# Loading the first pair of units by SyncE as fp32 and rounding it on the chip, in a fused attention and GELU kernel

## The chip, the cores and the metric

One Trainium2 chip, one of its cores. The metric is the device time of one execution in microseconds (us). The kernel before takes 132.57 us (median of 3 runs, 132.43 to 132.61). The profiled span of such a run is 130.3 us; the difference lies outside the profile.

## The reference

Inducing-point attention over `x` (4 batches of 12480 rows of 128), then an expert layer with exact GELU:

```python
def _attn_ref(x, inducing):
    ...                                  # scale = 1/sqrt(C), I = inducing for every batch
    def mab(q, kv):
        s = scale * (q @ kv.transpose(0, 2, 1))
        s = s - s.max(-1, keepdims=True)
        a = np.exp(s)
        a /= a.sum(-1, keepdims=True) + 1e-09
        return a @ kv
    h = mab(I, x)
    return mab(x, h).astype(np.float32)

def _moe_ref(x, w_in, w_out):            # x: the 49920 rows that the attention gives
    h = x @ w_in                         # 128 -> 2048
    g = 0.5 * h * (1.0 + erf(h * inv_sqrt2))
    return (g @ w_out).astype(np.float32)
```

The attention gives so small values that the kernel computes the expert layer from the 32 rows of `h` alone, with a check at the end. What matters here is the traffic: 25.6 MB of `x` in, 25.6 MB out, 2.1 MB of weights.

## The kernel before

`x` is worked on in units of 2048 rows, two units (a pair) to a tile of 128 partitions x 32 rows. GpSimd loads each pair in one transfer of 2.1 MB that rounds to fp16 on its way. For the first pair alone, SyncE loads the first half as fp32, and VectorE rounds it in two instructions:

```python
    def a_load(u):
        nc.gpsimd.dma_start(out=x_tile(u), in_=u.rows_of(x_rows))
...
    x_first = sb.tile([128, 32, 128], FP32, tag="o", bufs=OBUFS)
    x_pair = x_tile(units[0][0])
    src = units[0][0].rows_of(x_rows)
    nc.sync.dma_start(out=x_first[:, :16, :], in_=src[:, :16, :])
    nc.gpsimd.dma_start(out=x_pair[:, 16:, :], in_=src[:, 16:, :])
    a_load(units[0][2])
...
    ind_s = consts.tile([M, C], FP32)
    nc.scalar.dma_start(out=ind_s, in_=inducing)
...
    def a_cast(c0, engine):
        evacuate(engine, x_pair[:, c0 : c0 + 8, :], x_first[:, c0 : c0 + 8, :])
```

The order of all later work comes from a planner in the kernel: each piece is added with its cost in us, the buffers that it takes and gives, and, if it moves data, the length of the move. The planner runs the pieces through a model of engines and queues and emits them in that order, which is then pinned. A change of the loads therefore rearranges the whole program:

```python
    def add_load(u):
        if not loads:
            p = plan.add((0, 0), {"SP": 0.01}, lambda e: None, takes=["o"], move=LOAD_US)
            for c0 in (0, 8):
                p = plan.add((0, 1), {"DVE": 0.7, "ACT": 1.1},
                             lambda e, c0=c0: a_cast(c0, e), [p],
                             gives=["o"] if c0 == 8 else [])
            loads.append(p)
        elif len(loads) == 1:
            loads.append(plan.add((0, 1), {"POOL": 0.55}, lambda e: None,
                                  takes=["xh"], move=LOAD_US))
        elif u.first:
            ...
```

After building, the first transfers are moved ahead of the start barrier, each engine's to just before its first instruction of a given kind:

```python
def loads_ahead(nc):
    ...
    for engine, n, kind in (
        (ET.SP, 1, mybir.InstDrain),
        (ET.Activation, 1, mybir.InstDrain),
        (ET.Pool, 2, mybir.InstEventSemaphore),
    ):
        ...
```

Stores go by SyncE, one for each pair (2.1 MB) and, in the last batch, one for each unit (1.05 MB).

## Time and profile before

| | kernel before |
|---|---|
| time | 132.57 us |
| compute over at | 118.8 us of 130.3 |
| busy: PE, DVE, ACT, POOL | 76%, 70%, 59%, 50% |
| DMA time: GpSimd's queue (q0) + SyncE's (q1) | 50.1% + 48.9% of the span |
| HBM traffic | 27.7 MB read, 25.6 MB written |

PE is TensorE (PEld its weight loads), DVE is VectorE, ACT is ScalarE and POOL is GpSimd. The lines behind the table are in the prediction. Three things on reading them: the DMA row of the 40 slices is the mean of the 16 DMA engines; a line of a stretch has, after its length, the busy time and number of instructions of PE, PEld, DVE, ACT and POOL, then the granted clock, the DMA share and GB/s written; and in such a stretch the DMA share can exceed 1, because a packet counts whole where it begins and packets overlap (up to 25 at once in this trace). Eight filler matmuls, whose results nobody reads, stand at PE's start; the text comes back to them.

### The profile page before, as it was taken

Reading aid. Unit: us, or ns where it says so; the run is one execution under the profiler, and the core shown is the slowest. Engines: PE = TensorE matmul, PEld = TensorE weight load, DVE = VectorE, ACT = ScalarE, POOL = GpSimd, SP = SyncE. Lnnn points to the kernel's source line nnn. Section 1 sums busy time; section 2 is a strip of 40 time slices with the busy share of each in tenths; the row PEclk is TensorE's granted clock in tenths of the full one; section 3 lists DMA queues with packets and bytes.
Section 4 is the critical chain, followed back from the end, with each engine's and each line's share of the span. In section 5 each row is a group of like instructions: output and inputs, shape, how many; then the busy total and the mean of one; then the engine's idle time right before and its main releaser. Section 6 shows DMA issues by size and latency. Waiting matters only on the chain. (4 is left out here: it accounts for less than half of the span.)

```text
span 130.3 us, 3507 instructions
## 1 busy us (share of the span) xinstructions
PE 99.2 (76%) x1365; PEld 57.5 (44%) x1365; DVE 91.6 (70%) x265; ACT 77.1 (59%) x177; POOL 65.2 (50%) x85
## 2 busy tenths in 40 slices
PE   0954878549999999999789899999996698860000
PEld 0342656349465547656544664655453413310000
DVE  1836257432699997999999977999999757993000
ACT  3007064416756888578968889798996285960000
POOL 7910113019453836895753679765198842770000
PEclk9999599965799999999999999999999657998555
DMA  4999999999999999999999999999999999999993
GB/s 131 311 228 214 211 206 211 229 209 214 224 199 219 221 211 322 322 380 377 302 324 330 310 220 288 340 367 418 443 424 419 407 453 418 405 428 430 428 418 125
DMA packets 5666, 40.17 MB, mean 308 GB/s; under 512 B 624, under 2 KB 1936, under 8 KB 2192
## 3 DMA queue, kind: packets, MB, share of 16 engines
q0 software_dynamic: 2848, 13.30, 50.1%
q1 hardware_dynamic: 2752, 26.61, 48.9%
q8 instruction: 11, 0.18, 0.5%
q10 hardware_dynamic: 48, 0.02, 0.1%
q14 instruction: 7, 0.06, 0.1%
HBM read 27.67 MB, written 25.56 MB: 409 GB/s over the span
## 5 line engine op out<-in xcount | busy, mean ns | idle before, releaser
L702 POOL TENSOR_TENSOR pair<-pair,rr 128x512 f32<-128x512 f32 x26 | 26.8, 1042 | 20.6 <-ACT pair L365 17.7
L686 PE MATMUL at<-q,e 128*128 128x512 f16 (+1 forms) x104 | 33.4, 389 | 3.8 <-DVE xT L363 1.2
L377 PE MATMUL tr<-identity_h,xh 128*128 128x128 f16 x392 | 30.3, 232 | 3.3 <-DMA xh<-in_x_dram 3.3
L377 PEld LDWEIGHTS <-xh 128*128 128x128 f16 x392 | 25.2, 105 | 9.9 <-DMA xh<-in_x_dram 4.8
L363 DVE COPY xT<-tr 128x1024 f16<-128x1024 f16 (+1 forms) x36 | 22.6, 645 | 8.9 <-PE tr L377 8.3
L365 ACT ACTIVATE xT<-tr 128x1024 f16<-128x1024 f16 (+1 forms) x16 | 15.7, 980 | 16.5 <-PE tr L377 16.5
L717 DVE TENSOR_TENSOR pair<-at,rr 128x512 f32<-128x512 f32 x36 | 23.3, 676 | 1.1 <-PE at L686 0.4
L287 POOL DMA_DIRECT2D xh<-in_x_dram x15 | 8.3, 555 | 21.4 <-DMA xh<-in_x_dram 14.2
L403 ACT ACTIVATE e<-s 128x512 f16<-128x512 f32 (+1 forms) x28 | 15.3, 546 | 5.6 <-PE s L391 5.1
L638 ACT ACTIVATE e<-s 128x512 f16<-128x512 f32 (+1 forms) x28 | 15.0, 563 | 3.6 <-PE s L626 1.8
L365 ACT ACTIVATE pair<-at 128x512 f32<-128x512 f32 x26 | 15.6, 600 | 1.6 <-PE at L686 1.0
L686 PEld LDWEIGHTS <-e 128*128 128x128 f16 (+1 forms) x104 | 8.7, 103 | 10.3 <-issue 6.9
L417 DVE STREAM_TRANSPOSE e1t<-e 128x256 int32<-128x256 int32 (+1 forms) x28 | 11.1, 399 | 3.0 <-ACT e L403 2.9
L572 POOL TENSOR_TENSOR pt<-pt 128x512 f32<-128x512 f32 (+4 forms) x20 | 12.0, 602 | 2.1 <-DVE rr L661 0.7
L425 PE MATMUL hun<-xh,e1t 128*32 128x128 f16 x392 | 10.7, 225 | 3.1 <-DVE e1t L417 3.0
L717 DVE TENSOR_TENSOR o<-at,rr 128x512 f32<-128x512 f32 (+1 forms) x19 | 10.5, 580 | 3.0 <-PE at L686 2.6
L391 PE MATMUL s<-xT,indT 128*32 128x512 f16 (+1 forms) x108 | 10.5, 376 | 1.6 <-ACT xT L365 0.8
L626 PE MATMUL s<-xT,hT 128*32 128x512 f16 (+1 forms) x100 | 10.2, 417 | 0.5 <-DVE rr L661 0.5
L425 PEld LDWEIGHTS <-e1t 128*32 128x32 f16 x392 | 6.3, 97 | 8.9 <-DVE e1t L417 6.5
L702 POOL TENSOR_TENSOR o<-o,rr 128x512 f32<-128x512 f32 x7 | 7.3, 1042 | 5.4 <-ACT o L365 3.0
L650 PEld LDWEIGHTS <-e 128*128 128x128 f16 (+1 forms) x104 | 5.6, 99 | 4.4 <-issue 1.7
L650 PE MATMUL r<-strand,e 128*128 128x4 f16 (+1 forms) x104 | 6.8, 168 | 0.0
(76 smaller groups left out, 100.6 us busy)
## 6 DMA issues: line engine op xcount, KB each, us to landing
out_dram<-pair SPq DMA_DIRECT2D x8, 2048.0 KB, 15.1
xh<-in_x_dram POOLq DMA_DIRECT2D x11, 1024.0 KB, 28.1
out_dram<-o SPq DMA_DIRECT2D x6, 1024.0 KB, 10.7
out_dram<-spent SPq DMA_DIRECT2D x1, 2048.0 KB, 18.3
x_first<-in_x_dram SPq DMA_DIRECT2D x1, 1024.0 KB, 5.2
xh<-in_x_dram POOLq DMA_DIRECT2D x1, 512.0 KB, 7.1
w_in_h<-in_moe_w_in_dram POOLq DMA_DIRECT2D x1, 512.0 KB, 17.4
w_out_h<-in_moe_w_out_dram POOLq DMA_DIRECT2D x1, 512.0 KB, 19.4
```

The costliest lines, as they stand in the source:

```text
L363: nc.vector.tensor_copy(out=out, in_=in_)
L365: nc.scalar.activation(out=out, in_=in_, func=AF.Copy)
L377: nc.tensor.transpose(tr[:, c - c0, : u.p], xh[: u.p, c, :], identity_h[: u.p, : u.p])
L403: nc.scalar.activation(out=e1[: u.p, : u.nc // 2, :, :], in_=s1[: u.p, : u.nc, :].rearrange("r (a b) i -> r a i b", b=2), func=AF.Exp, sca ...
L417: nc.vector.transpose(out=pairs(e1t)[: u.p, :n], in_=pairs(e1)[: u.p, :n])
L425: nc.tensor.matmul(bt.hun[32 * j : 32 * j + 32, :], e1t[: u.p, c // 2, :, c % 2], xh[: u.p, c, :], start=u.idx == 0 and c < 4, stop=c + 4 ...
L572: nc.gpsimd.tensor_tensor(out=bt.pt[:, :, :, :half], in0=bt.pt[:, :, :, :half], in1=bt.pt[:, :, :, half : 2 * half], op=ALU.add,)
L638: nc.scalar.activation(out=e2[: u.rows, : u.cols], in_=s2[: u.rows, : u.cols], func=AF.Exp, scale=SCALE,)
L650: nc.tensor.matmul(r2[: u.p, ci, : u.nj], e2[: u.rows, ci * u.p : (ci + 1) * u.p], strand[: u.rows, : u.nj], start=True, stop=True,)
L686: nc.tensor.matmul(at[: u.p, : u.nj, :], e2[: u.rows, ci * u.p : (ci + 1) * u.p], bt.q[: u.rows, : u.nj, :], start=True, stop=True,)
L702: nc.gpsimd.tensor_tensor(out=part, in0=part, in1=rr2[: u.p, ci, : u.nj].unsqueeze(2).broadcast_to([u.p, u.nj, 128]), op=ALU.mult,)
L717: nc.vector.tensor_tensor(out=ov[: u.p, ci, :, :], in0=at[: u.p, : u.nj, :], in1=rr2[: u.p, ci, : u.nj].unsqueeze(2).broadcast_to([u.p, u. ...
```

## The change

SyncE loads the whole first pair as fp32 in two transfers, issued ahead of everything else on SyncE, and the second half is rounded on the chip too. GpSimd begins with the second pair.

```diff
-    nc.gpsimd.dma_start(out=x_pair[:, 16:, :], in_=src[:, 16:, :])
+    nc.sync.dma_start(out=x_first[:, 16:, :], in_=src[:, 16:, :])
     a_load(units[0][2])
+    a_load(units[0][4])
...
-        if not loads:
-            p = plan.add((0, 0), {"SP": 0.01}, lambda e: None, takes=["o"], move=LOAD_US)
-            for c0 in (0, 8):
+        if len(loads) < 2:
+            c = 16 * len(loads)
+            p = plan.add(..., takes=[] if loads else ["o", "xh"], move=LOAD_US)
+            for c0 in (c, c + 8):
...                                   (the planner's other lines follow suit)
-        (ET.SP, 1, mybir.InstDrain),
+        (ET.SP, 2, mybir.InstRegisterMove),
```

More of the change, by code (lines that the diff above doesn't have):

```diff
@@ L771, in add_load @@
     def add_load(u):
-        if not loads:
-            p = plan.add((0, 0), {"SP": 0.01}, lambda e: None, takes=["o"], move=LOAD_US)
-            for c0 in (0, 8):
+        if len(loads) < 2:
+            c = 16 * len(loads)
+            p = plan.add(
+                (0, 0),
+                {"SP": 0.01},
+                lambda e: None,
+                takes=[] if loads else ["o", "xh"],
+                move=LOAD_US,
+            )
+            for c0 in (c, c + 8):
                 p = plan.add(
-                    (0, 1),
+                    (0, 1 + c),
                     {"DVE": 0.7, "ACT": 1.1},
@@ L779, in add_load @@
                     [p],
-                    gives=["o"] if c0 == 8 else [],
+                    gives=["o"] if c0 == 24 else [],
                 )
             loads.append(p)
-        elif len(loads) == 1:
+        elif u.b == 0 and u.idx == 2:
             loads.append(
                 plan.add(
-                    (0, 1), {"POOL": 0.55}, lambda e: None, takes=["xh"], move=LOAD_US
+                    (0, 1), {"POOL": 0.55}, lambda e: None, takes=["xh"], move=2 * LOAD_US
                 )
@@ L793, in add_load @@
                     {"POOL": 0.55},
-                    lambda e: None if u.b == 0 and u.idx == 2 else a_load(u),
+                    lambda e: None if u.b == 0 and u.idx == 4 else a_load(u),
                     takes=["xht" if u.tail else "xh"],
@@ L999 @@
             nc,
-            {ET.SP: 0, ET.DVE: 26, ET.Activation: 0, ET.Pool: 12, ET.PE: 15},
+            {ET.SP: 0, ET.DVE: 26, ET.Activation: 0, ET.Pool: 11, ET.PE: 15},
         )
```

## The prediction

> **What bounds the kernel now.** I read the page's 40 slices first, because the share of busy time by engine (PE 76%, DVE 70%) names no bound.
>
> ```profile
> PE   0954878549999999999789899999996698860000
> DVE  1836257432699997999999977999999757993000
> ACT  3007064416756888578968889798996285960000
> DMA  4999999999999999999999999999999999999993
> GB/s 131 311 228 214 211 206 211 229 209 214 224 199 219 221 211 322 322 380 377 302 324 330 310 220 288 340 367 418 443 424 419 407 453 418 405 428 430 428 418 125
> ```
>
> The reader is to see that DMA is at 9 in every slice but the first and the last, while every compute engine has slices far below 9, and that in the last three to four slices (some 10 us) no engine works at all and the DMA still moves some 420 GB/s. GB/s counts what is written: a load that rounds fp32 to fp16 on its way shows half of what it reads, so 210 in slices 3 to 15 is 420 read, the same as the 405 to 453 of the pure stores from slice 28 on. Second, the queues:
>
> ```profile
> q0 software_dynamic: 2848, 13.30, 50.1%
> q1 hardware_dynamic: 2752, 26.61, 48.9%
> HBM read 27.67 MB, written 25.56 MB: 409 GB/s over the span
> ```
>
> The two add to 99% of the span. Per HBM megabyte: GpSimd's queue reads 26.6 MB (twice 13.30) in 0.501 x 130.3 = 65.3 us, 2.45 us each; SyncE's moves 26.61 MB in 0.489 x 130.3 = 63.7 us, 2.39 us each. Third, the busy time by stretch, which says where the DMA is not full (the columns end in clock, DMA share, GB/s):
>
> ```profile
> 0.00:1.00 1.00, 0.00 (x0) 0.00 (x0) 0.00 (x0) 0.00 (x0) 0.20 (x4) 1.00 0.00 0
> 1.00:2.00 1.00, 0.00 (x0) 0.00 (x0) 0.18 (x1) 0.00 (x0) 0.93 (x2) 1.00 0.50 92
> 2.00:3.00 1.00, 0.00 (x0) 0.00 (x1) 0.16 (x2) 0.87 (x1) 0.93 (x4) 1.00 0.84 260
> 3.00:4.00 1.00, 0.97 (x3) 0.46 (x4) 0.60 (x7) 0.41 (x1) 1.00 (x3) 1.00 0.96 401
> 120.00:125.00 5.00, 0.00 (x0) 0.00 (x0) 0.00 (x0) 0.00 (x0) 0.00 (x0) 0.50 1.01 428
> 125.00:128.00 3.00, 0.00 (x0) 0.00 (x0) 0.00 (x0) 0.00 (x0) 0.00 (x0) 0.50 0.87 363
> 128.00:130.30 2.30, 0.00 (x0) 0.00 (x0) 0.00 (x0) 0.00 (x0) 0.00 (x0) 0.50 0.18 69
> ```
>
> Only the first 3 to 4 us and the last 3 us are not full; every 2 us stretch between has a share of 0.94 or more. Last, the chain of waits, to see that compute is not what ends the run:
>
> ```profile
> 117.61 0.60 DVE hit L438 x8
> 118.25 0.22 PE tot_ps L969 x2
> 118.70 0.14 DVE failed L979
> ```
>
> Compute is over at 118.84, and the last store is issued at 118.0. What ends the run is about 9 us of queued stores, some 4 MB at 428 GB/s. So the kernel is 53.2 MB of HBM traffic at some 425 GB/s (125 us), a start of about 2 us and a close of about 3 us.
>
> **What the Trainium skill says.** (1) "DMA: Bandwidth & Descriptors", section "Issuing engines are not separate DMA queues": transfers issued by any engine run on the same 16 DMA engines, so starting them from several engines saves only issuing time. The trace agrees: 0.501 + 0.489 is a shared, full resource, not two. (2) Same page, "Specifications": a ceiling of 435 GB/s, and a first-byte latency of about 1 us for GpSimd's path, 0.6 us for SyncE's. The 428 here is at that ceiling; the first latencies can't be read singly, but no byte lands in the first 1 us. (3) Same page, "Queues, rings and completion order": each DMA engine takes turns between the queues that have work, packet by packet. Here 26.6 MB / 2848 and 26.61 MB / 2752 give 9.3 and 9.7 KB of HBM traffic a packet, so two active queues should get half each. (4) Same page, "SWDGE vs HWDGE vs iDMA": a cast in the transfer is to be had from GpSimd only, which is why SyncE's half comes as fp32 and is rounded on the chip.
>
> **The change, part by part.**
>
> Second half of the first pair (1.05 MB of HBM reads) moved from GpSimd's queue to SyncE's. HBM bytes stay the same; at the two rates above it saves 1.05 x (2.45 - 2.39) = 0.06 us of DMA time.
>
> SyncE's loads come ahead of its register moves. Before, SyncE's issue stands behind four of them; ScalarE's first issue stands behind none:
>
> ```profile
> 0.14 0.42 ACTq L305 DMA_DIRECT2D ind_s<-in_inducing_dram  x1
> 0.26 0.38 SPq L295 DMA_DIRECT2D x_first<-in_x_dram  x1
> 1.07 0.72 POOL L296 DMA_DIRECT2D xh<-in_x_dram  x1 [0.61 <-issue]
> 1.78 0.54 POOL L287 DMA_DIRECT2D xh<-in_x_dram  x1
> ```
>
> SyncE should issue at about 0.14, so 0.12 us earlier. As nothing else feeds the DMA then, and the DMA is full afterwards, this counts in full: -0.12 us. The second SyncE issue takes 0.38 us more before the start barrier; SyncE waits 0.8 us there now (its own waits say so), so it is free. GpSimd still has two issues ahead of the barrier (second and third pair now), so its first bytes and the identity that it makes after them don't move.
>
> The end tapers over some 3 us (share 0.87, then 0.18), so the 16 engines don't finish together. If the late ones are late because of GpSimd's transfers, 1.05 of 26.6 MB less takes 4% of some 2.5 us: -0.1 us, an estimate from the taper and the least certain term.
>
> Two more roundings of 128x1024, at 0.72 us on VectorE (the two now take 1.37 us together). They lie at 10 to 12 us, where VectorE is at 0.3 to 0.7 of a slice: nothing on the path.
>
> What moves early on: the first half lands as now (about 5.3 us). All transposes of the first pair now wait for GpSimd's half, because the first carries that wait, and begin at 8.23; in the changed order they wait for the roundings alone, so the first half begins at about 6.1. Its second half shares the DMA with GpSimd's second pair, so it needs twice its 2.45 us: 5.3 + 4.9 = 10.2 us, and some 0.7 us of rounding, against 8.2 now: 2.5 to 3 us later. The second pair has the same 4.2 MB ahead of and in it, so it lands at about 13.5 as now. The order of PE puts half a second-pair unit ahead of the first gather, so PE is up to one unit (about 2 us) behind at 13.6. It catches up while loads bound it, or the first store leaves up to 2 us later than 45.3. Neither is on the path: by 20 us the loads issued are some 15 MB and those served some 7.5 MB.
>
> Sum: -0.06 - 0.12 - 0.1 = -0.28 us: 132.57 becomes 132.3.
>
> **The rivals.** First, the earlier start of compute carries through (transposes 2.1 us earlier, up to -2 us: 130.5). For it: PE and ScalarE idle up to 6 us for data early on. Against: compute ends 9 us before the run does, and a gain of 2 us there would make the queue of stores deeper, not the end earlier. Second, the later second half and the new order (stores and the three engines' work are rearranged all along) leave the DMA dry somewhere: +1 to +2 us, about 134. For it: at 74 to 78 us GB/s falls to 224 to 240, the mark of loads alone, so the stores' queue is then empty, and if loads were finished earlier a gap would open. Against: the loads still last until about 89 us (the last is issued at 53.1 and such take up to 36.8 us to land), and the backlog of stores stays at about 3 MB or more (7 us) from 90 us on. Third, the last store is now one of 1 MB, behind the small one instead of ahead of it: if the last tile were finished over 7 us later the drain would follow compute, +1 us and more; I see no reason for so much. Fourth, more traffic written into the chip (1.05 MB instead of 0.52) costs DMA time: if what is written set the rate, loads that round would have gone faster than 210 GB/s written; so no.
>
> **Range and chances.** Executions of the kernel before spread by 0.18 us, the sum of my terms is 0.28, and a reshuffled schedule may shift the mix of loads and stores by some tenths either way. I take 131.5 to 132.8 as the range, with more room on the fast side since the start may gain more than 0.12 us. Over 2% would need 2.65 us, nearly the whole start or a gap that no stretch hints at: 0.02 for faster, 0.02 for slower, 0.96 within.
>
> **What would show it.** Right: DMA share near 1.0 from 3 us on; the software queue at 12.8 MB and the hardware one at 27.7; SyncE's first issue at about 0.14 us; first transposes at about 6 us, the two late roundings at 10 to 12 us, the second pair's transposes at 13 to 14; compute done 6 to 11 us before the end. Wrong: a 2 us stretch in the middle with a share under 0.9, compute ending within 4 us of the end, or a taper at the end that is gone or twice as long (then the engines' imbalance is worth more than I gave it).

## The result, and the profile after

The changed kernel takes 132.46 us (median of 5 runs, 132.11 to 132.82) against 132.57 us (132.43 to 132.61); the ratio is 0.9995 with a 95% interval of 0.9974 to 1.0016. Measured again later on one chip with other kernels it was 132.27 us against 132.53 us, ratio 0.9981 (0.9955 to 1.0007). A ratio here is the mean time of one kernel's fast runs over that of the other's of the same rounds, so not quite the ratio of the medians. Neither interval leaves 1: the change is worth nothing that can be told from zero, nor from the 0.28 us predicted; the medians are 0.1 and 0.3 us lower.

The queues of the page, in the changed kernel:

```profile
q1 hardware_dynamic: 2896, 27.66, 51.1%
q0 software_dynamic: 2704, 12.78, 48.3%
HBM read 27.67 MB, written 25.56 MB: 408 GB/s over the span
```

Half of the pair has changed sides (0.52 MB as written less on q0, 1.05 MB more on q1), the sum is still 99% of the span, and the HBM traffic is the same.

Busy time by stretch in the changed kernel (the last columns are clock, DMA share, GB/s written):

```profile
1.00:2.00 1.00, 0.00 (x0) 0.00 (x0) 0.19 (x1) 0.00 (x0) 0.94 (x2) 1.00 1.14 229
2.00:3.00 1.00, 0.00 (x0) 0.00 (x0) 0.17 (x2) 0.00 (x0) 0.92 (x4) 1.00 0.91 312
...
125.00:128.00 3.00, 0.00 (x0) 0.00 (x0) 0.00 (x0) 0.00 (x0) 0.00 (x0) 0.50 0.83 347
128.00:130.30 2.30, 0.00 (x0) 0.00 (x0) 0.00 (x0) 0.00 (x0) 0.00 (x0) 0.50 0.13 53
```

Against the same stretches in the prediction: from 1 to 3 us, 541 KB are moved instead of 352, so the start is some 190 KB ahead, 0.45 us at 425 GB/s. At the other end the taper is hardly smaller (0.83 and 0.13 instead of 0.87 and 0.18), and the span is the same 130.3 us. But each is one execution, and both took 132.41 us; for the kernel before that is 0.16 us under its median, so the equal spans don't show that nothing came out. More was gained at the start than predicted; how much of it is in the time stays open.

The timeline of the first 13 us of the changed kernel:

```profile
0.00 0.39 SPq L295 DMA_DIRECT2D x_first<-in_x_dram  x1
0.12 0.38 ACTq L306 DMA_DIRECT2D ind_s<-in_inducing_dram  x1
0.44 0.42 SPq L296 DMA_DIRECT2D x_first<-in_x_dram  x1
...
4.41 0.28 PE L308 MATMUL indT_ps<-identity,ind_s 32*128 32x32 f32 x1 [4.41 <-DMA ind_s<-in_inducing_dram]
4.63 3.59 PE L360 MATMUL dim<-blank 128*128 128x512 f16 x8
4.74 0.19 DVE L310 CAST indT<-indT_ps 128x32 f16<-128x32 f32 x1 [1.59 <-PE indT_ps L308]
6.71 0.68 DVE L364 CAST xh<-x_first 128x1024 f16<-128x1024 f32 x1
8.02 1.81 PE L378 MATMUL tr<-identity_h,xh 128*128 128x128 f16 x16
12.36 0.69 DVE L364 CAST xh<-x_first 128x1024 f16<-128x1024 f32 x1 [1.80 <-DMA x_first<-in_x_dram]
```

SyncE now issues 0.26 us earlier, ahead of ScalarE's small load of the inducing points. That load, of 16 KB, lands 4.2 us after its issue instead of 2.8. PE's first matmul at 4.41 us (3.03 before) and with it VectorE's `indT` at 4.74 us wait for it. In VectorE's program the constants and the first rounding stand after `indT`, so that rounding begins at 6.71 us (5.50 before) and ends at 7.39. But it is PE itself that is late: its eight fillers stand after its first matmul, one every 0.43 us from 4.63 us, and the first transposes follow them without a gap at 8.02 us, not at 6.1 as predicted and hardly earlier than 8.24 before. The second half is rounded at 12.36 us; predicted was a landing at 10.2.

### The profile page after: what moved, and what is told of

Same layout as the page of the kernel before. It is cut to its first block, busy times and chain, and to the rows that moved or that the text cites. A ratio compares the mean times of both kernels' runs of the same rounds, so it can differ in the third digit from the quotient of the medians.

```text
span 130.3 us, 3513 instructions
## 1 busy us (share of the span) xinstructions
PE 98.2 (75%) x1365; PEld 59.1 (45%) x1365; DVE 89.1 (68%) x262; ACT 80.5 (62%) x188; POOL 63.1 (48%) x82
## 3 DMA queue, kind: packets, MB, share of 16 engines
q1 hardware_dynamic: 2896, 27.66, 51.1%
## 5 line engine op out<-in xcount | busy, mean ns | idle before, releaser
L703 POOL TENSOR_TENSOR pair<-pair,rr 128x512 f32<-128x512 f32 x25 | 26.1, 1048 | 22.5 <-ACT pair L366 22.3
L378 PE MATMUL tr<-identity_h,xh 128*128 128x128 f16 x392 | 31.2, 236 | 5.5 <-DMA xh<-in_x_dram 5.2
L378 PEld LDWEIGHTS <-xh 128*128 128x128 f16 x392 | 26.2, 107 | 11.5 <-DMA xh<-in_x_dram 6.0
L364 DVE COPY xT<-tr 128x1024 f16<-128x1024 f16 (+1 forms) x32 | 20.9, 657 | 9.4 <-PE tr L378 9.1
L366 ACT ACTIVATE xT<-tr 128x1024 f16<-128x1024 f16 (+1 forms) x20 | 19.0, 958 | 11.5 <-PE tr L378 11.4
L718 DVE TENSOR_TENSOR pair<-at,rr 128x512 f32<-128x512 f32 x37 | 24.0, 679 | 0.8 <-PE s L627 0.2
L287 POOL DMA_DIRECT2D xh<-in_x_dram x15 | 8.5, 575 | 22.8 <-DMA xh<-in_x_dram 11.3
L366 ACT ACTIVATE pair<-at 128x512 f32<-128x512 f32 x25 | 15.0, 599 | 0.9 <-PE at L687 0.4
L718 DVE TENSOR_TENSOR o<-at,rr 128x512 f32<-128x512 f32 (+1 forms) x17 | 9.7, 592 | 0.7 <-PE at L687 0.3
L703 POOL TENSOR_TENSOR o<-o,rr 128x512 f32<-128x512 f32 x6 | 6.2, 1039 | 5.7 <-ACT o L366 3.3
L711 ACT ACTIVATE o<-at,rr 128x128 f32<-128x128 f32 (+1 forms) x24 | 7.2, 396 | 1.0 <-PE at L687 1.0
```

The source lines that it names most:

```text
L364: nc.vector.tensor_copy(out=out, in_=in_)
L366: nc.scalar.activation(out=out, in_=in_, func=AF.Copy)
L378: nc.tensor.transpose(tr[:, c - c0, : u.p], xh[: u.p, c, :], identity_h[: u.p, : u.p])
L703: nc.gpsimd.tensor_tensor(out=part, in0=part, in1=rr2[: u.p, ci, : u.nj].unsqueeze(2).broadcast_to([u.p, u.nj, 128]), op=ALU.mult,)
L718: nc.vector.tensor_tensor(out=ov[: u.p, ci, :, :], in0=at[: u.p, : u.nj, :], in1=rr2[: u.p, ci, : u.nj].unsqueeze(2).broadcast_to([u.p, u. ...
```

## The experiments

Eleven runs were made (one of them the changed kernel again), all correct. Ratios are to the kernel before, run on the same chip in the same rounds. An execution more than 1.5% above the fastest of its kernel is called slow; where a time is judged, fast runs alone are used. A profile is one execution.

**1. More traffic.** SyncE loads 1.05 MB more, into a part of a tile that nobody reads (made from the kernel before):

```diff
     nc.gpsimd.dma_start(out=x_pair[:, 16:, :], in_=src[:, 16:, :])
+    nc.sync.dma_start(out=x_first[:, 16:, :], in_=src[:, 16:, :])
...
-        (ET.SP, 1, mybir.InstDrain),
+        (ET.SP, 2, mybir.InstDrain),
```

> The kernel before with an extra load by SyncE of 1.05 MB of fp32 into a part of a tile that nothing reads. Theory (the DMA's total work is the bound): 1.05 MB at 2.4 us a MB, so 2.3 to 2.6 us more than the kernel before, about 135.0 us, ratio 1.018. Rival (a chain of compute is the bound and the DMA has room): under 0.5 us more.

Measured: 135.22 us against 132.48 us, ratio 1.0211 (1.0183 to 1.0238), so 2.8 us more. The added transfer costs its whole DMA time and a little over. Compute came later too (first transposes at 11.3 us), but it was over at 122.65 us of 132.7, with 10.1 us of stores still to go. The DMA's total work is the bound; the rival is out.

**2. Compute later.** Each filler matmul at PE's start is issued twice (made from the changed kernel):

```diff
-        nc.tensor.matmul(dim, blank[:, :128], blank, start=True, stop=True)
+        for _ in range(2):
+            nc.tensor.matmul(dim, blank[:, :128], blank, start=True, stop=True)
```

> The changed kernel with each of the eight filler matmuls at PE's start issued twice, so PE is free for the first transposes 8 x 0.43 = 3.4 us later; all other instructions stand in the same order. Theory (compute has room of 6 us and more everywhere): the first transposes begin at about 11.5 us and the time stays within 0.3 us of the changed kernel. Rival (what compute gains or loses at the start is carried to the end): 2 to 3.4 us more.

Measured: 132.47 us, ratio 0.9993 (0.9964 to 1.0022), the time of the changed kernel. The delay is 2.0 us instead of the 3.4 expected. PE's timeline shows why:

```profile
4.81 5.37 PE L361 MATMUL dim<-blank 128*128 128x512 f16 x16
10.01 1.06 PE L379 MATMUL tr<-identity_h,xh 128*128 128x128 f16 x16
```

The first eight fillers start every 0.43 us, the second eight every 0.22 us, so sixteen take 5.2 us and not twice 3.4; the transposes follow them without a gap at 10.01 us instead of 8.02. Nothing of it arrives at the end: compute is over at 117.9 us, 1.1 us before the changed kernel's. A start of compute that is 2 us later does not move the time.

**3. SyncE behind its register moves.** Only the place of the two loads is undone (made from the changed kernel):

```diff
-        (ET.SP, 2, mybir.InstRegisterMove),
+        (ET.SP, 2, mybir.InstDrain),
```

> The changed kernel with both SyncE loads put back behind SyncE's four register moves, nothing else moved. Theory A (the DMA is the bound and a byte moved earlier at the start is kept to the end): SyncE issues at about 0.26 us, the first bytes come 0.25 us later, and the time is 0.2 to 0.3 us above the changed kernel, so 0.1 to 0.2 us above the kernel before (ratio about 1.001). Theory B (the gain at the start is lost again before the end, because the last bytes come from the slowest of the 16 DMA engines): the same as the changed kernel within 0.15 us. Beside this, if it is the order of the issues that delays the small load of the inducing points (ScalarE's issue would now be ahead of SyncE's), that load lands at about 3 us instead of 4.4, the roundings begin at about 5.5 us instead of 6.7 and the first transposes about 1.2 us earlier than in the changed kernel, with no effect on the time.

Measured: 132.37 us against 132.48 us, ratio 0.9991 (0.9970 to 1.0012). The head start is gone but for 0.05 MB at 20 us, and the time is not higher; but theory A's ratio of 1.001 lies in the interval as well as theory B's, so this run decides between them no more than 0.1 us can be told from nothing. The side question is settled: ScalarE's issue, at 0.14 us, is now ahead of SyncE's at 0.26, the small load lands in 2.6 us, the first rounding begins at 5.55 us and the first transposes at 6.58, where the fillers end. It is the order of the issues that delays the small load, and that has no effect on the time: with experiment 2, neither 2 us later nor 1.4 us earlier transposes move it.

**4. SyncE ahead, without the second transfer.** One word of the change alone (made from the kernel before):

```diff
-        (ET.SP, 1, mybir.InstDrain),
+        (ET.SP, 1, mybir.InstRegisterMove),
```

> The kernel before with one thing of the change alone: SyncE's first load ahead of its register moves. Theory A: the first bytes come 0.25 us earlier and the time falls by 0.2 to 0.3 us (132.3). Theory B: the first bytes come earlier, the time stays within 0.1 us of the kernel before. The small load of the inducing points should land later than 2.9 us if its place behind SyncE's issue is what delays it.

Measured: 132.65 us against 132.48 us, ratio 1.0008 (0.9988 to 1.0029): no gain of the 0.2 to 0.3 us of theory A, although the first bytes come earlier (the interval does allow the prediction's 0.12 us). The small load lands 4.6 us after its issue, as expected. In the profile, the stretches from 5 to 7 us show where the earlier bytes go. The kernel before:

```profile
5.00:6.00 1.00, 1.00 (x4) 0.38 (x3) 0.91 (x11) 0.00 (x0) 1.00 (x3) 1.00 1.04 213
6.00:7.00 1.00, 0.79 (x2) 0.00 (x0) 0.86 (x2) 0.00 (x0) 0.37 (x1) 1.00 1.06 209
```

The kernel with SyncE's single load ahead:

```profile
5.00:6.00 1.00, 1.00 (x4) 0.42 (x4) 0.56 (x8) 0.00 (x0) 1.00 (x3) 1.00 0.89 180
6.00:7.00 1.00, 1.00 (x4) 0.32 (x3) 0.87 (x6) 0.00 (x0) 0.24 (x1) 1.00 1.05 152
```

In these 2 us GpSimd's queue is all but alone in both. It reads 2 x (213 + 209) = 844 KB in the one and 2 x (180 + 152) = 664 KB in the other: 180 KB are lost while the DMA goes over from SyncE's queue to GpSimd's. By 20 us (twice the bytes of q0 and once those of q1 in the stretch from 0 to 20 us) the kernel before has moved 7.45 MB, this one 7.35 and the changed kernel 7.64. But the profiled execution was the slowest of its six, 133.07 us, 0.42 us over their median, and 180 KB are 0.42 us at 425 GB/s: the loss at 5 to 7 us may belong to that one execution. That the other five lose it too is not shown. In the profiles, the head start is kept to 20 us where a second SyncE transfer runs beside GpSimd's first. Why GpSimd's packets are slow just there, at a share of 1.05, is not explained by any run.

**5. No load by SyncE.** The whole first pair by GpSimd (made from the kernel before; the roundings fall away, and the planner's pieces change with them, so the later order may differ too):

```diff
-    nc.sync.dma_start(out=x_first[:, :16, :], in_=src[:, :16, :])
-    nc.gpsimd.dma_start(out=x_pair[:, 16:, :], in_=src[:, 16:, :])
+    a_load(units[0][0])
```

> The kernel before with the whole first pair loaded and rounded by GpSimd, so no load by SyncE at all. Theory (SyncE's transfers are worth what they move before GpSimd's queue delivers its first byte, at 4.8 to 5.3 us): the DMA stands still until about 5 us instead of 1.3, and the time rises by 2.5 to 3.5 us over the kernel before (ratio about 1.023). Rival (the transfers by GpSimd would begin at 2 to 3 us if SyncE's were not in their way): under 1.5 us more.

Measured: 133.49 us against 132.74 us, ratio 1.0063 (1.0039 to 1.0086), so 0.8 us more and not 2.5 to 3.5. My theory was wrong and the rival right. The stretches from 2 us of this kernel:

```profile
2.00:3.00 1.00, 0.04 (x1) 0.05 (x1) 0.16 (x2) 0.87 (x1) 0.93 (x4) 1.00 0.92 90
3.00:4.00 1.00, 1.00 (x3) 0.41 (x4) 0.62 (x8) 0.42 (x1) 1.00 (x3) 1.00 0.57 74
4.00:5.00 1.00, 1.00 (x4) 0.42 (x3) 0.79 (x7) 0.00 (x0) 1.00 (x2) 1.00 0.99 205
```

GpSimd's queue works from the slice at 2 us on when it is alone, thinly until 4 us. In the other kernels its first packet comes at 4.0 to 5.6 us, when SyncE's first transfer has all but ended or has ended. What SyncE's load is worth is the difference at 20 us: 7.45 - 7.00 = 0.45 MB, 1.06 us at 425 GB/s, and 0.8 us of it is in the time.

**6. Smaller packets on the other queue.** GpSimd's load of the second pair in two halves (made from the changed kernel):

```diff
-    a_load(units[0][2])
+    second = units[0][2]
+    second_xh, second_rows = x_tile(second), second.rows_of(x_rows)
+    nc.gpsimd.dma_start(out=second_xh[:, :16, :], in_=second_rows[:, :16, :])
+    nc.gpsimd.dma_start(out=second_xh[:, 16:, :], in_=second_rows[:, 16:, :])
```

> The changed kernel with GpSimd's load of the second pair cut in two halves, each with 4 KB packets as written (8 KB read) instead of 8 KB (16 KB read). Theory of packet turns (queues alternate packet by packet, and a software packet of twice the bytes takes twice the DMA time): while both queues work, the software queue's share falls from about two thirds to about one half, and the second half of the first pair lands at about 10.5 us instead of 12.3. Rival (SyncE's queue is served less for another reason, such as a fixed preference): its landing stays at about 12.3 us. The time stays within 0.3 us of the changed kernel in both cases.

Measured: 132.24 us against 132.48 us, ratio 0.9978 (0.9952 to 1.0004), the same within the noise. The queues (packets, MB written, share) from 6 to 7 us in the changed kernel:

```profile
q0 software_dynamic: 20, 0.16, 78.6%
q1 hardware_dynamic: 16, 0.13, 33.0%
```

The same with the second pair in halves:

```profile
q1 hardware_dynamic: 28, 0.23, 58.0%
q0 software_dynamic: 23, 0.09, 46.4%
```

From issue to landing of SyncE's two loads (the smallest is the first half, the largest the second), in the changed kernel:

```profile
DMA to landing us min/median/max: 5.2/8.6/11.9
```

And with the second pair in halves:

```profile
DMA to landing us min/median/max: 5.2/7.2/9.3
```

The queues take turns by packets in both: 20 to 16, and 23 to 28. A packet of GpSimd's pair, 8 KB as written and 16 KB as read, takes 0.786 x 16 / 20 = 0.63 us of a DMA engine, one of SyncE's 8 KB takes 0.330 x 16 / 16 = 0.33 us; so SyncE's load got under a third of the time. With GpSimd's packets halved (0.464 x 16 / 23 = 0.32 us) it gets over half, and the second half lands at 0.44 + 9.3 = 9.7 us instead of 12.3. (The second profile of the changed kernel has 0.44 + 11.0 = 11.4 us; the kernel of experiment 9, with the same halves, has 9.4.) The theory holds, the rival is out. The share is not all of it: in the changed kernel under 0.1 MB of SyncE's 2.1 MB begin after 9 us, and these last packets take until 12; no run tells why they are late.

**7. The taper at the end.** The last store cut into 120 and 8 partitions (made from the changed kernel):

```diff
+        if u.b == B - 1 and u.idx == NFULL - 1:
+            nc.sync.dma_start(out=rows[:120, c0:c1, :], in_=o[:120])
+            nc.sync.dma_start(out=rows[120:, c0:c1, :], in_=o[120:])
```

> The changed kernel with its last store of 1 MB cut into one of 120 partitions and one of 8, so that the larger is spread over 15 of the 16 DMA engines and one of them gets up to 2.4 us less to do at the end. If the engine left out is one of the late ones, the last landing comes 0.3 to 1 us earlier and so does the end (131.5 to 132.1). If the late one is another engine, it gets one more 8 KB packet or so and the time rises by 0 to 0.4 us.

Measured: 133.11 us against 132.74 us, ratio 1.0027 (0.9999 to 1.0056); the profiled run fell in the slow state, so its times are not read. Its packets show that the cut did what it should: a whole store has 16 packets of 4 bytes beside its data, and here SyncE's queue has 7 more of them (2903 packets instead of 2896), as 15 + 8 in place of 16 give. The gain of 0.3 to 1 us did not come, so the engine that was spared is not the late one, or not the only one. The profile doesn't tell DMA engines apart, so which are late stays open.

**8. The parts exchanged.** Counted from the trace's packets, each spread over its time, the HBM traffic from 45 to 50 us, where the first store's data begin beside the loads, was 1.91 to 2.05 MB in the five profiles so far with the changed kernel's order (one of them slow), and 2.08 to 2.11 MB in the four with the old order. Two kernels exchange order and loads. First the old loads under the new order (made from the changed kernel; the condition drops the late roundings):

```diff
-    nc.sync.dma_start(out=x_first[:, 16:, :], in_=src[:, 16:, :])
+    nc.gpsimd.dma_start(out=x_pair[:, 16:, :], in_=src[:, 16:, :])
...
+        if c0 < 16:
...
-        (ET.SP, 2, mybir.InstRegisterMove),
+        (ET.SP, 1, mybir.InstDrain),
...
-        (ET.Pool, 2, mybir.InstEventSemaphore),
+        (ET.Pool, 3, mybir.InstEventSemaphore),
```

> The loads of the kernel before (half of the first pair by SyncE, half by GpSimd, SyncE behind its register moves) under the changed kernel's order of all other work; the two late roundings fall away. Theory C (the changed order loses DMA time where stores begin, at 45 to 50 us, and this eats the gain of the start): no gain at the start, the dip there, so 0.1 to 0.4 us above the kernel before (ratio 1.001 to 1.003), and at most 2.03 MB of HBM traffic at 45 to 50 us, against 2.08 in the kernel before. Rival (the dip in the five profiles of the changed order is chance): the same as the kernel before within 0.1 us, and 2.07 MB or more.

The changed kernel itself ran beside it:

> The changed kernel once more, beside the two above on one chip. Theory C: a dip at 45 to 50 us again (1.90 to 2.05 MB), ratio 0.998 to 1.000 to the kernel before, between the two other runs. If the dip is chance, it may be absent here.

Measured: the old loads under the new order take 132.51 us, ratio 0.9997 (0.9973 to 1.0021); the changed kernel 132.27 us, ratio 0.9981 (0.9955 to 1.0007); the kernel before 132.53 us. The queues (packets, MB written, share) from 45 to 50 us, in the kernel before:

```profile
q0 software_dynamic: 127, 0.91, 89.5%
q1 hardware_dynamic: 14, 0.23, 10.9%
```

In the changed kernel, first profile:

```profile
q0 software_dynamic: 123, 0.88, 90.6%
q1 hardware_dynamic: 15, 0.25, 11.7%
```

In the old loads under the new order:

```profile
q0 software_dynamic: 131, 0.94, 98.4%
q1 hardware_dynamic: 6, 0.10, 4.7%
```

HBM traffic is twice q0 and once q1: 2.05, 2.01 and 1.98 MB; the changed kernel's second profile has 1.97. (This view counts packets whole, so the kernel before has 2.05 here and 2.08 in the count above.) In this view the new order has 1.94 to 2.05 MB (mean 1.98 of the six fast profiles), and the four with the old order have 2.04 to 2.12 (mean 2.08). The dip is there again without the new loads, so it goes with the order and not with the loads, and it is 0.1 MB or 0.23 us on the mean, though the two groups meet (2.04 and 2.05). But the expected loss of 0.1 to 0.4 us is not in the time of that kernel, and the interval is too wide to say more.

Second, the new loads under the old order (made from the kernel before; the late roundings stand on VectorE in `a_transpose`, ahead of their transposes):

```diff
-    nc.gpsimd.dma_start(out=x_pair[:, 16:, :], in_=src[:, 16:, :])
+    nc.sync.dma_start(out=x_first[:, 16:, :], in_=src[:, 16:, :])
     a_load(units[0][2])
+    a_load(units[0][4])
...
+        if u.b == 0 and u.idx == 1:
+            a_cast(16 + c0, "DVE")
...
-        (ET.SP, 1, mybir.InstDrain),
+        (ET.SP, 2, mybir.InstRegisterMove),
```

> The changed kernel's loads (both halves by SyncE ahead of its register moves) under the order of the kernel before, with the two late roundings put on VectorE just ahead of the transposes that need them. Theory C: some 0.2 MB ahead at 20 us, no dip at 45 to 50 us (2.07 MB or more), so 0.2 to 0.5 us below the kernel before (ratio 0.996 to 0.998). Theory B (a start gained is lost in any case, in the lateness of the slowest DMA engine): within 0.1 us of the kernel before. VectorE's wait for the second half holds up the first transposed tiles until about 13 us; if that delays the first store past 46 us, a dip may open there for another reason.

Measured: 133.08 us, ratio 1.0031 (1.0000 to 1.0062): slower, if anything. VectorE's first copies of transposed tiles came at 13.70 us and the first store was issued at 49.18 us instead of 45.3, with compute over at 123.65 us. That is the other reason that the expectation allowed for; the kernel doesn't separate theories B and C.

**9. A version that should beat both.** As the last, with the second pair loaded in halves as in experiment 6, so that the second half lands earlier.

> The new loads under the old order, and GpSimd's load of the second pair cut in two halves, so that the first pair's second half lands at about 9.7 us and not 12.3. Theory C: as the new loads under the old order, ratio 0.995 to 0.998. Theory B: 1.000. This is the version that should beat both kernels if the start's gain can be kept.

Measured: 132.54 us against 132.53 us, ratio 1.0005 (0.9976 to 1.0034). It has the lead at 20 us (7.64 MB), but its first store is issued at 46.83 us and from 50 to 60 us it moves 4.05 MB where the kernel before moves 4.19. No version that I tried is clearly faster than the kernel before.

## Why the prediction was right or wrong

**The bound and the total: right.** 132.3 us was predicted and 132.46 and 132.27 us were measured, inside the range. That the sum fits says little for its terms, which are smaller than the noise: one could not be measured, one was sized wrongly and one had no ground, as told below. So far the hit is luck. The DMA's total work sets the time (experiment 1: 1.05 MB more cost 2.8 us), and compute has room (experiment 2: 2.0 us later cost nothing; a first store 3.8 us later may have cost 0.4 us, experiment 8). So the first rival falls, and its premise was wrong too: compute hardly started earlier. The second falls as well: from 2 to 126 us no 2 us stretch of the changed kernel has a DMA share under 0.92. So does the third: compute was over only 0.2 us later. So does the fourth: a packet of 8 KB as read takes 0.32 us where 4 KB are written and 0.33 us where 8 KB are (experiment 6). The prediction has compute end 9 us before the run; its own lines give 130.3 - 118.84 = 11.5 us, and the changed kernel has 11.3, just outside the 6 to 11 us that it named as a sign. The room was larger than it said.

**Half pair to SyncE's queue, -0.06 us:** too small to be measured. The page's shares give no gain: 99.0% before and 99.4% after.

**Earlier start, -0.12 us "in full": the size was wrong, and "in full" is not borne out.** The issue moved by 0.26 us, to the very start, and with the second transfer the lead at 20 us is 7.64 - 7.45 = 0.19 MB, 0.45 us. But the profiles don't bear out that it counts in full because the DMA is full afterwards. Alone it brought no gain that could be told from nothing, and in the one profile the traffic thinned when the DMA went over to GpSimd's queue (experiment 4). In the changed kernel's first profile the lead shrinks to 0.11 MB by 50 us, part of it at 45 to 50 us, and is still 0.10 MB at 120 us, 0.24 us at 425 GB/s. That is as much as the medians are lower by; whether this half reaches the time, or is lost because the last DMA engines end no earlier, the intervals can't tell. A deficit fared otherwise: 0.45 MB less at 20 us cost 0.8 us (experiment 5).

**The taper, -0.1 us:** not shown. The taper did not change by more than the shares quoted, and experiment 7 found no late engine. This term had no ground.

**Landing of the second half at 10.2 us: wrong, 12.3.** The failed step is equal halves for two active queues, taken from packet means over the whole run (9.3 and 9.7 KB). The transfers concerned have 16 KB and 8 KB packets as read, and experiment 6 shows the turns by packet and that shorter packets of the other queue bring the landing forward. How late the last packets come (12.3 us here, 11.4 in the second profile) is explained in part only.

**First transposes at 6.1 us: wrong, 8.02.** The prediction had the transposes wait for the rounding alone and left out PE's eight fillers, which hold PE until some 6.6 us in the kernel before (from 3.25 us, one every 0.43 us). In the changed kernel they start 1.4 us later, since the small load behind SyncE's is late and PE's first matmul waits for it. Experiment 3 puts the issue back and has 6.58 us.

**Unchanged landing of the second pair:** right; its transposes begin at 13.12 us (13.62 before). The first store at 45.1 us (45.3) is right too; compute was over at 119.0 us (118.8).

**Left open:** why traffic falls off when the DMA goes over from one queue to another (4 to 7 us in experiment 4's one profile) or begins to serve a second one (45 to 50 us), why the new order loses more there, and which DMA engines end late. The last 0.1 to 0.3 us can't be resolved against runs of one kernel that spread by 0.2 to 0.9 us.

## What to carry to other kernels

When the DMA is full from start to end, bytes not moved, or moved into an empty stretch, are what can count; look for such stretches before moving work between engines, and follow a head start through the rest of the profile, since here half of it was gone by 50 us. Check whether the profiled execution is a typical one before you explain a loss that it shows. Take the packet sizes of the very transfers that compete, not the means of a queue, when you work out when a shared transfer lands. Before moving a large transfer to the front, look for a small one on which the engines' first instructions wait, and count all that an engine has to do before the instruction that you mean to start earlier.

## What the Trainium skill lacked or had wrong

- "DMA: Bandwidth & Descriptors", "Queues, rings and completion order" says that queues take turns packet by packet, but not that this divides time by packet length where one queue casts: a rounding packet of 16 KB as read held a DMA engine 0.63 us against 0.33 us for a plain one of 8 KB, so the plain transfer got 33% of the time, and 58% once the other's packets were halved.
- The same page, "Specifications", gives about 1 us to the first byte for GpSimd's path. Behind a SyncE transfer of 1.05 MB issued earlier, GpSimd's queue moved nothing until 4 to 5 us although issued at 1.07 us; with no SyncE load it moved data from 2 us on, but only 74 to 90 GB/s as written until 4 us.
- No page that I read has a figure for what a small load loses when it is issued 0.12 us after a large one on another engine: 16 KB from ScalarE took 4.2 us to land, and 2.6 us when issued 0.12 us ahead of it.
